# Loads of q, k and v issued as one transfer for each batch instead of one for a pair of batches

## The chip, the cores and the metric

The kernel runs on one core of a Trainium2 chip. The metric is the device time of one execution in microseconds (us). Three runs of the kernel before gave 429.69, 429.71 and 430.25 us; their median, 429.71 us, is what a forecast is held against.

## What is computed

Lightning attention with a decay per head, and a feed-forward layer in which each token goes to one of eight experts (4 batches, 8 heads, 768 positions, head dimension 64; 3072 tokens of width 512; 8 experts with 1024 hidden units):

```
for b in range(nb):
    sl = slice(b * block, (b + 1) * block)
    qb, kb, vb = (q[:, :, sl], k[:, :, sl], v[:, :, sl])
    intra = np.einsum('bhic,bhjc->bhij', qb, kb) * Dmask[None]
    intra = np.einsum('bhij,bhjd->bhid', intra, vb)
    inter = np.einsum('bhid,bhde->bhie', qb * lam_pow[None], kv_state)
    out[:, :, sl] = intra + inter
    kb_dec = kb * rev_pow[None]
    kv_state = lam_block * kv_state + np.einsum('bhsd,bhse->bhde', kb_dec, vb)
...
logits = x @ w_gate
expert_idx = np.argmax(logits, axis=1)
...
for e in range(E):
    mask = expert_idx == e
    h = np.maximum(x[mask] @ w1[e], 0.0)
    out[mask] = gate_w[mask, None] * (h @ w2[e])
```

## The kernel before

**Stages.** The attention takes about the first 125 us, the experts the rest. The attention works in 12 steps, numbered 0 to 11 here: six blocks of 128 positions, and for each block two pairs of batches (`steps`). A step needs three tiles of 512 KB: q, k and v of its 128 positions, two batches and eight heads, with a position on each partition, so that a partition holds 16 rows of 256 bytes (2 batches by 8 heads). I call them q9, k9 and v9 for step 9.

**One step on TensorE (PE).** `turn_q` and `turn_k` transpose q and k (`tq`, `tk`, L244). `score` multiplies them (`sp`, L282). `attend_states` (`op`, L311), `grow` (`cp`, L350) and `attend` (`op`, L324) make the output and the new state; the last two read v. `to_sbuf` then copies `op` to `xT` on ScalarE (ACT, L336 and L342), and `logits` (`lgT`, L376) and `rows` (`tx`, L385) read `xT`. The order of these on PE is pinned; the scores of the next step stand between `op` L324 and `lgT`.

**Loads.** `load` (L102 to L118) issues the loads on SyncE's queue (SP). Step 0's q and k go as eight transfers of 128 KB (L115), each a batch and half of the heads. Everything else is one transfer of 512 KB (L117). `begin(i)` issues q and k of step i+4 and v of step i+3. There are five tiles for each name (`homes`: three of the pool, two in the room of later weights), so a load waits until the step five before it is done with its tile. After the last of them SP issues the first half of the first expert's w1 (L1154), and the second half (L1159) once the early list of tokens has been read.

**Row stores.** When a step's rows are finished, `store_rows` (L395) writes 512 KB to `xs` in HBM with a transfer that ACT issues. For step s it stands on ACT behind the last `kT` copy of step s+2 and ahead of the `xT` copies of step s+1. I call it store s. ACT works in order: as long as the issue of a store waits, what stands behind it on ACT waits too. Behind store 7 stands first `rank_in` (L454), a copy for the places of step 7's tokens in the lists.

**Completion counters.** Transfers of SP and of ACT share eight counters, DMAHW0 to DMAHW7, and take them in turn in the order in which the program was scheduled. A transfer waits for the one that had its counter before, that is for the transfer eight places ahead of it, until that one has landed.

Of the kernel before, what the change touches and what calls it, by code (L numbers as in the profile page):

```python
# [23 lines left out]
def kernel(  # L24
# [29 lines left out]
    nc = tc.nc  # L54
# [47 lines left out]
    def load(i, names, first=False):  # L102

        if i >= len(steps) or (i, names[0]) in loaded:
            return
        n, b0 = steps[i]
        parts = (slice(0, H // 2), slice(H // 2, H)) if first else (slice(0, H),)
        for name in names:
            loaded[i, name] = homes[name][i % len(homes[name])]
        for hs, name in itertools.product(parts, names):  # L110
            src = {"q": q, "k": k, "v": v}[name][b0:b0 + 2, hs, n * C:(n + 1) * C, :]
            to = loaded[i, name]
            if first:
                for b in range(2):
                    nc.sync.dma_start(out=to[:, b, hs], in_=src[b].rearrange("h s d -> s h d"))  # L115
            else:
                nc.sync.dma_start(out=to.rearrange("p b h d -> p (b h) d"),  # L117
                                  in_=src.rearrange("b h s d -> s (b h) d"))  # L118


    lam_bc = const.tile([P, H], F32, name="lam_bc")

    nc.scalar.dma_start(out=lam_bc, in_=lam.partition_broadcast(P))
    load(0, "qk", True)
    load(0, "v")
    load(1, "qk")
    load(1, "v")
    load(2, "qk")
# [48 lines left out]
    for h in itertools.chain(range(0, H, 2), range(1, H, 2)):  # L177
        nc.vector.tensor_tensor_scan(
            out=decay[:, h % 2, h // 2, :], data0=lam_bc[:, h:h + 1].to_broadcast([P, C]),
# [14 lines left out]
    def pick(per_e, e):  # L194

        if isinstance(e, int):
            return per_e[e]
        return per_e[bass.ds(e, 1)].squeeze(0)
# [994 lines left out]
    def stores(i):  # L1193
        if i == len(steps) - 2:
# [5 lines left out]
                            in_=moe_w_gate.rearrange("(c p) e -> p c e", p=P)))  # L1200
# [195 lines left out]
    with tc.If(most > 0):  # L1396
        with tc.For_i(0, E, 1) as i:
            tiles = nc.values_load(beyond[0:1, bass.ds(i, 1)], min_val=0, max_val=max(MORE))
            with tc.If(tiles > 0):
# [19 lines left out]
                    out=slots, out_offset=bass.IndirectOffsetOnAxis(ap=end_i, axis=0),  # L1419
                    in_=none.bitcast(F32), in_offset=None)  # L1420
                w1t, w2t = load_weights(e)
                with tc.For_i(0, tiles, 1) as r:
# [4 lines left out]
                        out=m.list[:, 0, :], in_=pick(by_e, e)[bass.ds(r * P + r0, P), :])  # L1427
# [32 lines left out]
```

## Time and profile before

| what | us |
|---|---|
| median of three runs | 429.71 |
| profiled execution, its time | 430.3 |
| its span in the trace | 428.5 |
| attention, start to the first expert's first product (`ph`, L613) | 0 to 123.9 |
| loads of q, k and v: first and last issue on SP | 0.77 and 101.3 |
| row stores 0 to 11 on ACT | 25.2 to 123.1 |

The profiled execution took 430.3 us, of which the trace shows 428.5; 1.8 us lie around the span. It stands 0.6 us above the median. On SP a row of the timeline shows how long the issue of a transfer held the queue; "to landing" counts from the start of that issue until all of the transfer has arrived. "DMA share" is the mean busy share of the core's 16 DMA engines; as packets of one engine overlap in the records, it can be above 1.

### The profile page before, as it was taken

Reading aid. Unit: us, or ns where it says so; the run is one execution under the profiler, and the core shown is the slowest. Engines: PE = TensorE matmul, PEld = TensorE weight load, DVE = VectorE, ACT = ScalarE, POOL = GpSimd, SP = SyncE. Lnnn points to the kernel's source line nnn. Section 1 sums busy time; section 2 is a strip of 40 time slices with the busy share of each in tenths; the row PEclk is TensorE's granted clock in tenths of the full one; section 3 lists DMA queues with packets and bytes.
Section 4 is the critical chain, followed back from the end, with each engine's and each line's share of the span. In section 5 each row is a group of like instructions: output and inputs, shape, how many; then the busy total and the mean of one; then the engine's idle time right before and its main releaser. Section 6 shows DMA issues by size and latency. Waiting matters only on the chain.

```text
span 428.5 us, 9723 instructions
## 1 busy us (share of the span) xinstructions
PE 416.9 (97%) x3775; PEld 393.6 (92%) x3776; DVE 261.7 (61%) x578; ACT 173.5 (40%) x319; POOL 256.6 (60%) x210
## 2 busy tenths in 40 slices
PE   8999999999799999999999999999999999999995
PEld 7888988989688898999999999999999999999964
DVE  7656656776565647585557757554775655556454
ACT  3365445556442324460554154335414525331141
POOL 4242656472333467498929866794876778559143
PEclk9999999999999999999999999999999999999999
DMA  8999989989976866969358956865985996673221
GB/s 174 209 242 230 229 208 230 249 183 230 255 259 160 302 111 164 333 161 390 55 122 179 364 84 155 313 186 112 251 297 81 149 348 163 150 210 46 30 78 64
DMA packets 164545, 83.06 MB, mean 194 GB/s; under 512 B 145923, under 2 KB 145959, under 8 KB 164496
## 3 DMA queue, kind: packets, MB, share of 16 engines
q1 hardware_dynamic: 155024, 63.21, 61.3%
q0 software_dynamic: 5536, 12.88, 9.8%
q10 hardware_dynamic: 3936, 6.31, 4.3%
q8 instruction: 31, 0.51, 0.5%
q14 instruction: 18, 0.15, 0.1%
HBM read 58.96 MB, written 12.72 MB: 167 GB/s over the span
## 4 chain that ended last, share of the span: by engine, by line
PE 83%; DMA 7%; DVE 3%; ACT 2%; issue 2%; POOL 1%; SPq 1%; POOLq 0%; DVEq 0%; ACTq 0%
PE p L737 26%; PE p L943 26%; PE ph L613 5%; PE sp L282 5%; PE p L783 4%; PE op L324 4%; DMA v_in<-in_v_dram 4%; PE cp L350 2%; DMA xg<-xs,list 2%; PE tx L385 2%; PE op L311 2%; PE tk L244 2%; PE tq L244 2%; DMA xg<-xs,list_0a 1%; PE p L791 1%
## 5 line engine op out<-in xcount | busy, mean ns | idle before, releaser
L540 POOL DMA_INDIRECT out_dram<-o_room,list x24 | 25.5, 1065 | 54.0 <-DMA decay<-planes_q 23.6
L737 PE MATMUL p<-xgT,w1t 128*128 128x209 f32 (+6 forms) x224 | 41.3, 327 | 0.3 <-DVE u_kT L627 0.3
L289 DVE TENSOR_TENSOR mt<-sp,decay 128x512 f32<-128x512 f32 x48 | 29.8, 683 | 17.2 <-PE sp L282 17.2
L748 ACT ACTIVATE hT<-hT 128x418 f32<-128x418 f32 (+6 forms) x56 | 27.9, 520 | 29.1 <-DVE hT L745 28.1
L737 PEld LDWEIGHTS p<-xgT,w1t 128*128 128x128 f32 x224 | 37.1, 189 | 1.0 <-DVE u_kT L627 0.6
L625 ACT COPY u_qT<-p 128x418 f32<-128x418 f32 (+6 forms) x14 | 6.7, 478 | 70.2 <-PE p L737 70.2
L943 PE MATMUL p<-hT,w2t 128*128 128x209 f32 (+5 forms) x192 | 33.6, 328 | 0.0
L943 PEld LDWEIGHTS p<-hT,w2t 128*128 128x128 f32 x192 | 32.0, 189 | 0.0
L473 POOL DMA_INDIRECT slots<-entry,slot_i x24 | 23.7, 990 | 13.1 <-PE tl L399 6.7
L534 POOL DMA_INDIRECT xg<-xs,list x25 | 25.6, 1024 | 6.7 <-issue 6.4
L745 DVE TENSOR_TENSOR hT<-p,u_kd 128x418 f32<-128x418 f32 (+6 forms) x28 | 15.6, 559 | 19.7 <-PE p L737 19.6
L282 PE MATMUL sp<-qT,kT 64*128 64x128 f32 x384 | 25.0, 279 | 0.9 <-DVE qs_room L258 0.9
L272 POOL TENSOR_TENSOR kd<-k_in,kdec 128x512 f32<-128x512 f32 x12 | 12.5, 1052 | 22.1 <-issue 6.6
L662 POOL TENSOR_TENSOR s_q<-w1t 128x1024 f32<-128x1024 f32 x7 | 16.5, 2362 | 15.1 <-DVE t_xT L722 12.5
L282 PEld LDWEIGHTS sp<-qT,kT 64*128 64x128 f32 x384 | 22.6, 188 | 3.2 <-issue 1.9
L592 ACT COPY xgT<-decay 128x1672 uint16<-128x1672 uint16 (+6 forms) x7 | 13.6, 1942 | 20.9 <-DMA decay<-planes_k 20.9
L613 PE MATMUL ph<-xgT,w1t 128*128 128x256 f32 (+1 forms) x128 | 21.6, 329 | 0.1
L613 PEld LDWEIGHTS ph<-xgT,w1t 128*128 128x128 f32 x128 | 19.3, 191 | 1.9 <-DVE xgT L604 0.3
L988 ACT ACTIVATE o_room<-o_room,list 128x512 f32<-128x512 f32 (+6 forms) x22 | 14.1, 710 | 16.9 <-DMA o_room<-qs_room 16.9
L336 ACT COPY xT<-op 128x512 f32<-128x512 f32 x12 | 7.0, 585 | 34.3 <-PE op L324 30.9
L737 PE MATMUL p<-t_xT,w1t 128*128 128x209 f32 (+6 forms) x112 | 20.6, 326 | 0.0
L737 PE MATMUL p<-st,s_q 128*128 128x209 f32 (+6 forms) x112 | 20.6, 326 | 0.0
(260 smaller groups left out, 1100.4 us busy)
## 6 DMA issues: line engine op xcount, KB each, us to landing
w2t<-in_moe_w_dram SPq DMA_DIRECT2D x8, 2048.0 KB, 12.2
w1t<-in_moe_w_dram SPq DMA_DIRECT2D x7, 2048.0 KB, 16.2
xs<-x_room ACTq DMA_DIRECT2D x12, 512.0 KB, 6.3
v_in<-in_v_dram SPq DMA_DIRECT2D x8, 512.0 KB, 8.3
o_room<-qs_room SPq DMA_DIRECT2D x76, 48.0 KB, 2.1
q_in<-in_q_dram SPq DMA_DIRECT2D x7, 512.0 KB, 9.1
k_in<-in_k_dram SPq DMA_DIRECT2D x7, 512.0 KB, 8.9
room<-in_q_dram SPq DMA_DIRECT2D x4, 512.0 KB, 8.7
```

What stands on the lines that cost most here:

```text
L244: pin(nc.tensor.transpose(t[:, i, b, :], src[:, b, h:h + 2, :], ident))
L282: m.scored = pin(nc.tensor.matmul(sp[u][:, i, b, :], lhsT=m.kT[s][halves[u], i, b, :], rhs=m.qT[s][halves[u], i, b, :], start=(i == 0 and ...
L289: nc.vector.tensor_mul(mt[:, u], sp[u], decay[:, u, s * HP // 2:(s + 1) * HP // 2].unsqueeze(2).to_broadcast(shp))
L324: pin(nc.tensor.matmul(out_at(m, b, u, hp), lhsT=m.v[:, b, 2 * hp + u, :], rhs=m.mt[hp // 2][:, u, hp % 2, b, :], start=(first and hp == 0 ...
L473: put = nc.gpsimd.indirect_dma_start(out=slots, out_offset=bass.IndirectOffsetOnAxis(ap=slot_i[:, i:i + 1], axis=0), in_=entry[:, n, bs[i] ...
L534: return nc.gpsimd.indirect_dma_start(out=dst, out_offset=None, in_=xs[:rows, :], in_offset=bass.IndirectOffsetOnAxis(ap=idx, axis=0))
L540: put = nc.gpsimd.indirect_dma_start(out=out, out_offset=bass.IndirectOffsetOnAxis(ap=idx, axis=0), in_=src, in_offset=None, bounds_check= ...
L613: nc.tensor.matmul(ph, lhsT=w1t[:, dc, fc * P:(fc + 1) * P], rhs=m.xgT[:, dc, :], start=(dc == 0), stop=(dc == DC - 1))
L737: nc.tensor.matmul(p[:, i, :], lhsT=lhs[:, dc, g, i * P:(i + 1) * P], rhs=rhs[:, dc, :], start=(dc == 0), stop=(dc == DH - 1))
L748: pin(nc.scalar.activation(outs[i][k], outs[i][k], ACT.Relu))
L783: nc.tensor.matmul(p, lhsT=x, rhs=y, start=(k == 0), stop=(k == 3))
L943: nc.tensor.matmul(p[:, c, :], lhsT=lhs[:, f, c * P:(c + 1) * P], rhs=rhs[:, f, :], start=(f == 0), stop=(f == FC // 2 - 1))
```

## The change

Each load that was one transfer of 512 KB becomes two of 256 KB, batch 0 and then batch 1, in the same place on SP. The 8 transfers of step 0's q and k stay as they are. So 34 transfers become 68. The rows moved, their size (256 bytes) and their places in SBUF are the same; within a transfer a partition now has 8 rows instead of 16.

```
             else:
-                nc.sync.dma_start(out=to.rearrange("p b h d -> p (b h) d"),
-                                  in_=src.rearrange("b h s d -> s (b h) d"))
+                for b in range(2):
+                    nc.sync.dma_start(out=to[:, b], in_=src[b].rearrange("h s d -> s h d"))
```

The order of the instructions on PE, VectorE, ACT and GpSimd stays as it was. What changes is SP's list, and which transfer had each counter before. Two places show it. The first is ACT around store 7, before, with the waits of each instruction in brackets:

```order
L254 COPY qT<-tq 128x512 [waits PE_49,Activation_49]
L411 ACTIVATE ex<-sh 128x16 [waits DVE_49]
L266 COPY kT<-tk 128x512 [waits PE_49,Activation_49]
L395 DMA xs<-x_room 128x2x512 [waits DMAHW3_49,Activation_49]
L454 COPY rank_in<-rank 128x24 [waits PE_49]
L336 COPY xT<-op_1627 128x4x128 [waits PE_49]
L342 COPY xT<-op_1628 64x4x128 [waits PE_49]
```

and now:

```order
L254 COPY qT<-tq 128x512 [waits PE_49,Activation_49]
L411 ACTIVATE ex<-sh 128x16 [waits DVE_49]
L266 COPY kT<-tk 128x512 [waits PE_49,Activation_49]
L395 DMA xs<-x_room 128x2x512 [waits DMAHW4_49,Activation_49]
L454 COPY rank_in<-rank 128x24 [waits PE_49]
L336 COPY xT<-op_1661 128x4x128 [waits PE_49]
L342 COPY xT<-op_1662 64x4x128 [waits PE_49]
```

Only the counter of the store has changed, from 3 to 4. Which load had it is to be read on SP. Before, q10 to v11 (`room_69` is the tile of v9):

```order
L117 DMA q_in<-in_q_dram 128x16x64 [waits DMAHW3_49,PE_49]
L117 DMA k_in<-in_k_dram 128x16x64 [waits DMAHW4_49,Pool_49]
L117 DMA room_69<-in_v_dram 128x16x64 [waits DMAHW5_49,PE_49]
L117 DMA q_in<-in_q_dram 128x16x64 [waits DMAHW7_49,PE_49]
L117 DMA k_in<-in_k_dram 128x16x64 [waits DMAHW0_49,Pool_49]
L117 DMA v_in<-in_v_dram 128x16x64 [waits DMAHW1_49,PE_49]
L117 DMA v_in<-in_v_dram 128x16x64 [waits DMAHW2_49,PE_49]
```

and now from k10's second half to v11's first:

```order
L118 DMA k_in<-in_k_dram 128x8x64 [waits DMAHW1_49,PE_49]
L118 DMA room_69<-in_v_dram 128x8x64 [waits DMAHW2_49,PE_49]
L118 DMA room_69<-in_v_dram 128x8x64 [waits DMAHW4_49,PE_49]
L118 DMA q_in<-in_q_dram 128x8x64 [waits DMAHW5_49,PE_49]
L118 DMA q_in<-in_q_dram 128x8x64 [waits DMAHW6_49,PE_49]
L118 DMA k_in<-in_k_dram 128x8x64 [waits DMAHW7_49,Pool_49]
L118 DMA k_in<-in_k_dram 128x8x64 [waits DMAHW0_49,PE_49]
L118 DMA v_in<-in_v_dram 128x8x64 [waits DMAHW1_49,PE_49]
L118 DMA v_in<-in_v_dram 128x8x64 [waits DMAHW2_49,PE_49]
L118 DMA v_in<-in_v_dram 128x8x64 [waits DMAHW3_49,PE_49]
```

Counter 3 belonged to q10 before store 7 took it; now store 7 takes counter 4 after the second half of v9. Counted the same way, stores 5, 6 and 8 wait for the second halves of q8, k9 and k11 (before: k7, v7 and an earlier store). The counter that is missing between v9's halves is store 6's, 3; v11's first half now waits for that store.

## The prediction

> **What bounds the kernel now.** I read the page first, for the shares and the chain that ended last.
>
> ```profile
> PE 416.9 (97%) x3775; PEld 393.6 (92%) x3776; DVE 261.7 (61%) x578; ACT 173.5 (40%) x319; POOL 256.6 (60%) x210
> PE 83%; DMA 7%; DVE 3%; ACT 2%; issue 2%; POOL 1%; SPq 1%; POOLq 0%; DVEq 0%; ACTq 0%
> ```
>
> PE is busy for 97% of the span, and the chain lies on it for 83%. A change of loads alone can gain only where PE waits for a load. The waits of PE up to 125 us and its timeline at the longest of them show how much that is.
>
> ```profile
> PE op L324 <- DMA v_in<-in_v_dram: 1.0, 1, 1.0
> PE cp L350 <- DMA v_in<-in_v_dram: 0.2, 1, 0.2
> ...
> 108.25 0.49 PE L244 MATMUL tk<-ident,k_in 128*128 128x128 f32 x3 [0.43 <-issue]
> 109.70 1.97 PE L324 MATMUL op<-mt,v_in 128*64 128x128 f32 x32 [0.96 <-DMA v_in<-in_v_dram]
> ```
>
> For the loads that the change touches PE waits 1.2 us in all: 0.2 us for v0 at the start and 0.96 us from 108.7, where step 10's `op` waits for v10 (step 0's q and k, for which it waits a little too, aren't changed). In the chain v10 is the late load that carries it, from its issue at 98.74 to 109.56:
>
> ```profile
> 95.28 0.57 PE lgT L376 x16
> 98.74 10.82 DMA v_in<-in_v_dram
> ```
>
> The next question is why v10 is late. The timeline of SP's queue and the landings of single transfers:
>
> ```profile
> 4.04 1.06 SPq L115 DMA_DIRECT2D k_in<-in_k_dram  x2
> 5.69 2.42 SPq L117 DMA_DIRECT2D q_in<-in_q_dram  x1
> 53.48 5.21 SPq L117 DMA_DIRECT2D q_in<-in_q_dram  x1
> 77.23 1.99 SPq L117 DMA_DIRECT2D room<-in_k_dram  x1
> 89.06 2.84 SPq L117 DMA_DIRECT2D room<-in_v_dram  x1
> 95.38 3.27 SPq L117 DMA_DIRECT2D k_in<-in_k_dram  x1
> 107.67 1.80 SPq L1154 DMA_DIRECT2D w1t<-in_moe_w_dram  x1
> ```
>
> ```profile
> q_in<-in_q_dram SPq DMA_DIRECT2D x1, 128.0 KB, 3.2
> k_in<-in_k_dram SPq DMA_DIRECT2D x1, 128.0 KB, 3.5
> k_in<-in_k_dram SPq DMA_DIRECT2D x1, 512.0 KB, 10.9
> room<-in_k_dram SPq DMA_DIRECT2D x1, 512.0 KB, 7.8
> room<-in_v_dram SPq DMA_DIRECT2D x1, 512.0 KB, 10.4
> k_in<-in_k_dram SPq DMA_DIRECT2D x1, 512.0 KB, 9.7
> ```
>
> (The transfers issued at 0.77, 4.59, 48.06, 77.23, 89.06 and 95.38; L115 issues one in 0.5 us.) q1's issue took until 8.11, when the last 128 KB had landed (4.59 + 3.5 = 8.09). q7's, 53.48 to 58.69, ended with k6's landing (48.06 + 10.9 = 58.96), two loads earlier; w1's, until 109.47, with v10's (98.74 + 10.82 = 109.56). So SP gets about two loads of 512 KB ahead and is then held until the older one has landed. Then one load is still queued on the engines, and the windows show that this does not always last:
>
> ```profile
> 10.00:17.00 7.00, 6.33 (x110) 5.40 (x107) 4.81 (x8) 1.77 (x4) 1.71 (x5) 1.00 1.31 208
> 17.50:18.00 0.50, 0.50 (x7) 0.33 (x5) 0.00 (x0) 0.50 (x2) 0.44 (x1) 1.00 0.62 143
> 24.50:25.50 1.00, 0.51 (x5) 0.27 (x3) 0.45 (x1) 1.00 (x3) 1.00 (x2) 1.00 0.56 127
> 39.50:40.50 1.00, 1.00 (x12) 1.00 (x10) 0.65 (x5) 1.00 (x4) 0.00 (x0) 1.00 0.42 96
> 48.50:50.00 1.50, 1.50 (x16) 1.50 (x15) 0.74 (x4) 1.50 (x4) 0.00 (x0) 1.00 0.37 86
> 57.50:61.00 3.50, 2.86 (x41) 2.47 (x43) 1.56 (x7) 2.71 (x7) 0.10 (x1) 1.00 0.31 71
> 73.00:74.00 1.00, 1.00 (x20) 0.83 (x17) 0.83 (x3) 0.10 (x1) 0.84 (x2) 1.00 0.47 109
> 78.00:79.00 1.00, 1.00 (x12) 1.00 (x11) 0.55 (x5) 1.00 (x4) 0.00 (x0) 1.00 0.73 167
> 87.00:89.50 2.50, 2.50 (x38) 2.33 (x39) 1.67 (x10) 2.50 (x8) 2.08 (x3) 1.00 0.50 115
> 93.50:95.00 1.50, 1.50 (x31) 1.50 (x30) 0.77 (x3) 1.36 (x3) 1.47 (x2) 1.00 0.61 139
> ```
>
> The last two columns are the DMA share and GB/s. With loads alone and a full queue the share is 1.31 at 208 GB/s; in nine dips it falls far below, down to 0.31. The queues of two windows say who works in a dip, and what came before it:
>
> ```profile
> q8 instruction: 1, 0.02, 5.5%
> ...
> q1 hardware_dynamic: 155, 0.04, 11.3%
> ```
>
> In 54.1 to 55.1 one packet of the program's own instructions took 5.5% of 16 engines, 0.9 us of one engine. In 58.5 to 60.0 only 11.3% of 16, some two engines' worth, moves loads: some engine is behind, SP is held by it, and the others are dry.
>
> **The change part by part.** *More issues.* 34 more at 0.5 us (L115's row) are 17 us of SP. From q1 on a load holds SP for 1.99 to 5.21 us in the rows above, so its second issue falls into time in which SP is held anyway: 0. If that cover were gone, 1 us of issue for 2 × 1.26 us of transfer still keeps up. v0's second half is issued 0.55 us later, under the 128 KB transfers that land until 8.09: 0, between -0.1 and +0.1.
>
> *Depth of the queue.* If SP's room is a number of rows, as the 128 KB transfers suggest (six were in flight, unheld), SP is freed when the oldest half has landed, and three halves are queued then, not one whole load: half a load, 256 KB, more, 1.26 us at 208 GB/s. The nine dips lost their length times (1 - share / 1.31): 0.26, 0.57, 0.68, 1.08, 2.67, 0.64, 0.44, 1.55 and 0.80, together 8.7 us. With each shortened by at most 1.26 us the stream is 7.0 us earlier by v9, 4.9 us by k9. If the room is a number of transfers, or the lagging engine sets the pace by itself, it is 0. I take 7.0, since the room for eight issues at the start is the nearest row.
>
> *Rate of halves.* The eight transfers of 128 KB were issued every 0.55 us, 238 GB/s, and the landing grew from 3.2 to only 3.5 us: they kept up with more than 208. I take the same rate for halves. In the Trainium skill, "DMA: Bandwidth & Descriptors", section "Rules for kernel authors", full bandwidth asks for 128 partitions and 1 MiB or more in a transfer, and small transfers should be merged; that speaks against halves. By it the stream would be slower and the time that of the second rival; the trace's 128 KB transfers do not bear it out.
>
> *PE's wait.* v10 would land at 102.6, so the 0.96 us go, -1.0. Next late is nothing: PE runs on through `op`, and what follows (0.43 us "issue") isn't a load. Everything behind is PE's chain and moves with it. Bounds: -1.6 with the 0.43 and v0's 0.2 gone too, 0 if v10 stays.
>
> *A new wait.* Stores on ACT now wait for loads that are half as far back. In the timeline of ACT:
>
> ```profile
> 79.95 0.37 ACTq L395 DMA_DIRECT2D xs<-x_room  x1
> 83.37 0.58 ACT L336 COPY xT<-op 128x512 f32<-128x512 f32 x1 [2.81 <-PE op L324]
> 89.38 0.59 ACT L266 COPY kT<-tk 128x512 f32<-128x512 f32 x1
> 92.24 0.37 ACTq L395 DMA_DIRECT2D xs<-x_room  x1
> 92.65 0.18 ACT L454 COPY rank_in<-rank 128x24 f32<-128x24 f32 x1 [2.68 <-DMA q_in<-in_q_dram]
> 93.12 0.59 ACT L336 COPY xT<-op 128x512 f32<-128x512 f32 x1 [0.29 <-PE op L324]
> 93.73 1.17 ACT L342 COPY xT<-op 64x512 f32<-64x512 f32 x2
> ```
>
> Store 7 was ready at 89.97 and already waited to 92.24, for q10. Behind it stand `rank_in` and `xT`, and PE's `lgT` waits for `xT`: 92.24 to 94.90 is 2.66 us, and `lgT` began at 95.28, so a store 7 up to 92.6 costs nothing. Now it waits for v9, which landed at 89.06 + 10.4 = 99.5, 6.9 us too late. 7.0 us from the dips, and up to 2.5 us as store 7's own 512 KB (at 208 GB/s) no longer go ahead of v9, just cover that: 0. Store 6 waits for k9, 85.0 before and 80.1 then; it is needed by 83.0. Store 8 waits for k11, 105.1 before and 98.1 then, and is ready at 98.96.
>
> Sum: 430.3 - 1.0 = 429.3 for an execution like the profiled one; against the median, **428.7 us**.
>
> **The rivals.** *ACT waits for v9.* With a gain g of the stream, store 7 goes at 99.5 - g, `lgT` is 6.9 - g late, and PE no longer waits for v10: 5.9 - g in all, slower than before when g is below 5.9. With half of the expected gain, 3.5, that is +2.4: 432.1. For it: the margin is thin, and a lagging engine may lag on. Against it: the dips are long enough.
>
> *Halves move no faster or worse,* by the rule on size. Then only store 7's own absence helps, g about 1: +4.9, 434.6. Against it: the 128 KB rows.
>
> *Nothing to measure.* g between 5.1 and 6.7, so that ACT's wait gives back what PE gains: 429.7. It also holds if v10 gains less than 0.9 us.
>
> **How the numbers follow.** Chances: forecast 0.43, ACT waits 0.25, slower halves 0.10, nothing to measure 0.22. A measurement here can tell about 0.2%, 0.86 us, from no change. The forecast's own range is 427.9 (-1.6, and 0.2 for the scatter of runs, which was 429.69 to 430.25 before) to 429.0. The range for all reaches to 433.6 (g = 2), leaving out most of the slower halves. The gain of 1.0 is hardly above 0.86, so 0.05 of the forecast counts as same, 0.38 as faster; of nothing to measure 0.15 is same, 0.03 faster, 0.04 slower; of the other two 0.34 slower, 0.01 same. Together 0.41 faster, 0.21 same, 0.38 slower.
>
> **What would show it.** Right: no wait of PE for v10; v9's second half landed by 92.6; the dips shorter; w1's first issue well ahead of 107.67. Wrong: a long wait of `rank_in` for a load of v, `lgT` behind it late by the same; or SP's issues of halves in which only one load is in flight.

## The result: slower, by store 7's wait

| kernel | median, us | lowest to highest | to the kernel before, 95% interval |
|---|---|---|---|
| before | 429.71 (5 runs) | 429.31 to 430.46 | |
| changed | 435.83 (5 runs) | 432.00 to 436.52 | 1.0119 [1.0091, 1.0147] |

The forecast was 428.7, with 433.6 as the upper end of its range. The change costs 6.1 us by the medians, 5.1 us by the ratio. The ratios, here and below, leave out single executions that ran more than 1.5% above the fastest of their kernel. The times of the change spread over 4.5 us where those of the kernel before spread over 1.2. The profiled execution is the fastest of the five: 432.0 us, span 430.2, and so 1.7 us above the one of before.

ScalarE (ACT) around store 7, after:

```profile
90.99 0.58 ACT L266 COPY kT<-tk 128x512 f32<-128x512 f32 x1
96.84 0.37 ACTq L395 DMA_DIRECT2D xs<-x_room  x1
97.25 0.18 ACT L454 COPY rank_in<-rank 128x24 f32<-128x24 f32 x1 [5.68 <-DMA room<-in_v_dram]
97.33 0.59 ACT L336 COPY xT<-op 128x512 f32<-128x512 f32 x1
```

ACT was done with `kT` at 91.57 and then did nothing until 96.84, when v9 had landed. The idle time stands at `rank_in`, since the issue of a transfer isn't counted as work; the wait is store 7's. TensorE (PE) meanwhile, before and then after:

```profile
93.22 2.06 PE L282 MATMUL sp<-qT,kT 64*128 64x128 f32 x32
95.21 0.64 PE L376 MATMUL lgT<-xT,gates 128*32 128x128 f32 x16
...
102.52 2.06 PE L282 MATMUL sp<-qT,kT 64*128 64x128 f32 x32
```

```profile
94.05 2.18 PE L282 MATMUL sp<-qT,kT 64*128 64x128 f32 x32
97.97 0.42 PE L376 MATMUL lgT<-xT,gates 128*32 128x128 f32 x8 [1.74 <-ACT xT L336]
99.16 0.42 PE L376 MATMUL lgT<-xT,gates 128*32 128x128 f32 x8 [0.77 <-ACT xT L342]
...
106.26 2.06 PE L282 MATMUL sp<-qT,kT 64*128 64x128 f32 x32
```

From the scores (`sp`) of step 9 to those of step 10 took 9.30 us before and 12.21 now, 2.9 more, of which 1.74 + 0.77 are waits of PE for `xT`. PE's wait of 0.96 us for v10 is gone from the list of waits, as forecast, and the first product of the experts began 1.9 us later than before, at 125.83.

The scores of step 9 stood 0.83 us later already (94.05 for 93.22). Part of that is store 6, which now waits for k9 and went at 84.26; PE waited for the second `xT` behind it:

```profile
84.26 0.37 ACTq L395 DMA_DIRECT2D xs<-x_room  x1
86.50 0.43 PE L376 MATMUL lgT<-xT,gates 128*32 128x128 f32 x8 [0.24 <-ACT xT L342]
```

The loads did not come forward. SP's queue after, and the windows of two of the dips that were counted before:

```profile
88.75 4.22 SPq L118 DMA_DIRECT2D room<-in_v_dram  x2
...
98.85 8.04 SPq L118 DMA_DIRECT2D v_in<-in_v_dram  x4
106.94 0.68 SPq L1154 DMA_DIRECT2D w1t<-in_moe_w_dram  x1
```

```profile
57.50:61.00 3.50, 3.50 (x50) 3.32 (x54) 2.13 (x7) 2.64 (x7) 0.77 (x1) 1.00 0.87 188
...
93.50:95.00 1.50, 1.50 (x28) 1.33 (x26) 0.36 (x1) 0.00 (x0) 1.30 (x3) 1.00 0.65 146
```

SP came to v9 at 88.75 (89.06 before) and was done with both halves at 92.97 (91.90 before); it came to w1 at 106.94 (107.67). The longest dip is filled (share 0.87 for 0.31), others came elsewhere: of the half microseconds from 12 to 100 us, 34 had a DMA share below 0.65 before, and 34 have it after. From 50 to 95 us the DMA engines moved as much as before, 219 GB/s for 216. First before, then after:

```profile
50.00:95.00 45.00, 44.36 (x824) 40.02 (x822) 30.59 (x91) 24.16 (x54) 26.36 (x30) 1.00 0.91 216
```

```profile
50.00:95.00 45.00, 44.22 (x815) 39.92 (x815) 31.83 (x84) 23.80 (x53) 25.57 (x29) 1.00 0.95 219
```

### The profile page after: what moved, and what is told of

The parts are those of the page before. It is cut to its first block, busy times and chain, and to the rows that moved or that the text cites. A ratio compares the mean times of both kernels' runs of the same rounds, so it can differ in the third digit from the quotient of the medians.

```text
span 430.2 us, 9789 instructions
## 1 busy us (share of the span) xinstructions
PE 417.7 (97%) x3775; PEld 393.9 (92%) x3776; DVE 260.6 (61%) x578; ACT 173.6 (40%) x319; POOL 255.9 (59%) x210
## 4 chain that ended last, share of the span: by engine, by line
PE 86%; DVE 4%; DMA 3%; SPq 2%; ACT 2%; issue 2%; POOL 0%; ACTq 0%; POOLq 0%; DVEq 0%
PE p L737 30%; PE p L943 26%; PE ph L613 5%; PE p L783 4%; PE sp L282 4%; PE op L324 3%; PE p L791 3%; PE tx L385 2%; PE op L311 2%; PE tq L244 2%; PE tk L244 2%; DMA room<-in_v_dram 2%; PE cp L350 2%; DMA k_in<-in_k_dram 2%; SPq L118 1%
## 5 line engine op out<-in xcount | busy, mean ns | idle before, releaser
L745 DVE TENSOR_TENSOR hT<-p,u_kd 128x418 f32<-128x418 f32 (+6 forms) x28 | 15.6, 559 | 19.7 <-PE p L737 18.8
L662 POOL TENSOR_TENSOR s_q<-w1t 128x1024 f32<-128x1024 f32 x7 | 16.5, 2359 | 15.3 <-DVE t_xT L722 12.5
L737 PE MATMUL p<-t_sd,w1t 128*128 128x209 f32 (+6 forms) x112 | 20.6, 326 | 0.0
```

What stands on the lines that cost most here:

```text
L662: return nc.gpsimd.tensor_tensor(out=o, in0=x, in1=y, op=ALU.subtract)
L737: nc.tensor.matmul(p[:, i, :], lhsT=lhs[:, dc, g, i * P:(i + 1) * P], rhs=rhs[:, dc, :], start=(dc == 0), stop=(dc == DH - 1))
```

## The experiments

The theory is called the counter theory below: store 7 on ACT now has the completion counter of v9's second half, waits for it, and holds `xT`, on which PE waits. Its rivals are that halves move slower, and that halves deepen the queue as the prediction had it. Each run was compared with the kernel before on the same chip; as chips differ (that kernel's median was 430.3 us beside e1 to e4, 426.9 to 427.3 beside the others), ratios are given. On which chip the first comparison ran is not on record.

| run | ratio to before, 95% interval |
|---|---|
| e5, e10: full change again | 1.0127 [1.0086, 1.0168], 1.0119 [1.0083, 1.0155] |
| e8: kernel before against itself | 1.0031 [1.0003, 1.0058] |
| e6: all halves but v10, store 7 free | 1.0042 [1.0018, 1.0066] |
| e7: full change, stores behind `xT` | 1.0031 [1.0008, 1.0054] |
| e1: halves up to step 8 | 1.0001 [0.9984, 1.0017] |
| e2: halves from step 9 on | 1.0001 [0.9986, 1.0015] |
| e3: whole loads, store 7 on v9's counter | 1.0039 [1.0008, 1.0070] |
| e4, e11: stores by GpSimd, halves and whole | 1.0046 [1.0032, 1.0059], 1.0028 [1.0005, 1.0052] |
| e9: full change and filler on PE | 1.0130 [1.0092, 1.0167] |
| e12: quarters | 1.0288 [1.0241, 1.0334] |
| e13: all halves but v8, store 6 free | 1.0148 [1.0126, 1.0170] |
| e14: whole loads, store 6 on k9's counter | 0.9993 [0.9974, 1.0012] |

Since e8 shows 0.3% between a kernel and itself, nothing under that is read as an effect.

**The wait taken away, the halves kept (e6, e7).** e6 leaves v10 whole. That is one transfer fewer ahead of store 7, which so gets the counter of store 6.

```
-                for b in range(2):
+            elif (i, name) != (10, "v"):
+                for b in range(2):
                     ...
+            else:
+                nc.sync.dma_start(out=to.rearrange("p b h d -> p (b h) d"), ...)
```

> The full change but for one load: v10 is whole again. That makes one transfer fewer ahead of store 7, whose counter then is that of store 6, landed long before; 67 of the 68 transfers stay halves or nearly so. Counter theory: store 7 goes at about 90.5, no wait of ACT for a load of v, 429.5 to 430.8 us. Slow-halves theory: as the full change, 432 us or more, with PE waiting for v10 for 2 us or more.

ACT in e6:

```profile
90.83 0.37 ACTq L398 DMA_DIRECT2D xs<-x_room  x1
91.78 0.18 ACT L457 COPY rank_in<-rank 128x24 f32<-128x24 f32 x1 [1.46 <-PE rank L451]
```

Store 7 goes at 90.83, ACT waits for PE and no longer for a load, and the loss is gone: 428.60 us where the full change beside it had 433.47. With 33 of 34 loads in halves the kernel is as fast as before, to what e8 can tell. Two smaller waits of the same kind are left in its profile: PE waited 0.70 us for the `xT` behind store 6 and 0.20 us for the one behind store 8. e7 gets there by another way: `store_rows` is called behind `to_sbuf`, so that the order of stores and loads changes too and store 7 has the counter of store 6.

```
-        if ahead:
-            with tc.issue_after(ahead.copied.ins):
-                store_rows(last)
...
         to_sbuf(cur)
+        if ahead and not swapped(cur):
+            with tc.issue_after(cur.turned.ins):
+                store_rows(last)
```

> The full change, and every row store up to store 9 is issued behind the xT copies of its step on ACT rather than ahead of them; store 7 then has the counter of store 6, and a store that waits no longer holds xT. Counter theory: the loss is gone, 429.5 to 430.8 us (428.7 if PE's waits for v10 and for xT both go). Slow-halves theory: 432 us or more.

It took 428.48 us. The forecasts were made for a chip with 430 us; by the ratios, 1.0042 and 1.0031 against 1.0127 for the full change, taking the wait away takes away the loss, to within the 0.3% of e8. In e7's profile an earlier store, issued at 78.45, held ACT for a load of v instead, and PE waited 1.92 us there; that the ratio is no higher with this wait in it shows how coarse the comparison is. As e6's interval reaches 1.0066, a small loss by the halves themselves is not excluded. Neither kernel beats the one before.

**The wait alone, without halves (e3).**

```
                 nc.sync.dma_start(out=to.rearrange("p b h d -> p (b h) d"), ...)
+                if i == 11 and name in "qk":
+                    for j in range(2 if name == "q" else 1):
+                        nc.sync.dma_start(out=shift[:1, j:j + 1], in_=lam.partition_broadcast(1)[:, :1])
```

> Whole loads as before; three transfers of 4 bytes are added on SP behind q11 and k11, for nothing but to shift the counters: store 7 now has the counter of v9 (whole). Counter theory: store 7 goes when v9 has landed, at about 99.4, some 7 us later than before; less the 2.7 us that are hidden and the 1 us that PE then no longer waits for v10, about 434 to 436 us. Slow-halves theory: there are no halves, so 429.7 us as before.

Eight of twelve times lay between 429.7 and 431.2, four between 432.8 and 436.4. The last four lie about where the counter theory asked for them (434 to 436), the eight about where the rival did (429.7). The granted clock on record was 0.991 to 0.996 in the four and 0.998 or more in the eight. The profiled execution, the fastest, shows how a short time can occur although store 7 waits:

```profile
94.27 0.37 ACTq L400 DMA_DIRECT2D xs<-x_room  x1
94.67 0.18 ACT L459 COPY rank_in<-rank 128x24 f32<-128x24 f32 x1 [4.31 <-DMA room<-in_v_dram]
```

```profile
93.20 2.14 PE L287 MATMUL sp<-qT,kT 64*128 64x128 f32 x32
95.39 0.43 PE L381 MATMUL lgT<-xT,gates 128*32 128x128 f32 x8
96.59 0.43 PE L381 MATMUL lgT<-xT,gates 128*32 128x128 f32 x8 [0.77 <-ACT xT L347]
```

Store 7 did wait for v9, 4.31 us long, but v9 landed at 94.27, and not at the 99.5 of the profile of before; PE lost 0.77 us. So one profile had shown one landing of several. None of the four long executions was profiled; that v9 landed later in them is not shown. e8 shows another landing without any change.

**The kernel before, once more (e8).**

> The kernel before, unchanged, for a second trace of it: how far the landing of v9 and the pace of the loads differ between two executions of one kernel. Counter theory: 430.0 us within 0.5; v9 lands anywhere between 94 and 100, and the time does not depend on it, since store 7 has the counter of q10. Slow-halves theory: 430.0 us, and every load is issued earlier by 1 us or more than in the halved kernels.

SP and the landing of v9 in e8, and its DMA from 50 to 95 us:

```profile
87.09 2.32 SPq L117 DMA_DIRECT2D room<-in_v_dram  x1
```

```profile
room<-in_v_dram SPq DMA_DIRECT2D x1, 512.0 KB, 7.2
```

```profile
50.00:95.00 45.00, 45.00 (x844) 40.73 (x842) 31.60 (x93) 24.29 (x55) 27.37 (x31) 1.00 1.00 232
```

v9 landed at 87.09 + 7.2 = 94.3, 5.2 us ahead of the first profile, with the same code, though perhaps on another chip; 232 GB/s for 216. This execution took 426.1 us and PE did not wait for v10. The twelve times of e8 spread from 426.0 to 431.4 without any wait for v9, so a wide spread alone does not point to that wait. The slow-halves theory expected loads issued earlier here than in the halved kernels; e13 below takes that up.

**One part of the change (e1, e2).** e1 has `elif i < 9:` ahead of the halves, e2 `elif i >= 9:`.

> Halves for steps 0 to 8, whole loads for steps 9 to 11, so that store 7 on ACT has the counter of q10 again, as before the change. Counter theory (the loss comes from ACT's store 7 waiting for the second half of v9, and halves change nothing in the pace of the loads): store 7 goes between 92 and 93, no wait of lgT in step 8, PE waits about 1 us for v10 again; 429.3 to 430.2 us. Slow-halves theory (halves move slower and put the whole stream of loads back): store 7 and v10 are late, 431.5 us or more. Deep-queue theory of the prediction (halves bring the stream forward): no wait for v10, 428.7 us.

> The other part alone: whole loads for steps 0 to 8, halves for steps 9 to 11 (18 transfers in place of 9); store 7 has the counter of the second half of v9, as in the change. Counter theory: store 7 goes at 96 to 100, lgT of step 8 is 2.5 to 6 us late, 432 to 436 us, about as the full change. Slow-halves theory: only a quarter of the loads are halves, so a quarter of the loss, 430.2 to 431.3 us.

In e1 store 7 went at 90.47, ahead of the 92 to 93 expected, PE did not wait for v10 although the counter theory said it would, and the time was 430.52 us: the time of the kernel before beside it (430.29), but just outside the counter theory's bounds of 429.3 to 430.2, and below the slow-halves theory's 431.5. In e2 the counter theory's number missed, 430.68 us for 432 to 436, and the slow-halves theory's held. Its ACT and PE:

```profile
94.08 0.41 ACTq L398 DMA_DIRECT2D xs<-x_room  x1
94.54 0.18 ACT L457 COPY rank_in<-rank 128x24 f32<-128x24 f32 x1 [2.62 <-DMA room<-in_v_dram]
```

```profile
97.84 0.43 PE L379 MATMUL lgT<-xT,gates 128*32 128x128 f32 x8 [0.36 <-ACT xT L345]
```

Store 7 waited for the second half of v9 as in the change, but that landed by 94.08, and PE lost 0.36 us. The wait is there; what it costs is set by when v9 lands.

**The change again, and PE's clock (e5, e10, e9).**

> The changed kernel once more, unchanged, beside the runs below on the same chip. Counter theory: its times spread as the landing of the second half of v9 does, between 430.5 and 436.5 us, and in the profiled execution store 7 goes when that half has landed; the time is about 430 us plus what store 7 is later than 94. Slow-halves theory: its times are all about 2 us or more above the next kernel's tail of the same halves, and near to those of the kernel in which only v10 is whole.

The profiled execution took 434.83 us. SP, the landing of v9's second half (issued at 90.5), ACT and PE:

```profile
89.55 2.69 SPq L118 DMA_DIRECT2D room<-in_v_dram  x2
```

```profile
room<-in_v_dram SPq DMA_DIRECT2D x1, 256.0 KB, 6.6
```

```profile
97.19 0.39 ACTq L395 DMA_DIRECT2D xs<-x_room  x1
97.61 0.18 ACT L454 COPY rank_in<-rank 128x24 f32<-128x24 f32 x1 [7.11 <-DMA room<-in_v_dram]
```

```profile
93.75 2.06 PE L282 MATMUL sp<-qT,kT 64*128 64x128 f32 x32
98.33 0.66 PE L376 MATMUL lgT<-xT,gates 128*32 128x128 f32 x8 [2.52 <-ACT xT L336]
99.53 0.65 PE L376 MATMUL lgT<-xT,gates 128*32 128x128 f32 x8 [0.54 <-ACT xT L342]
109.09 1.16 PE L282 MATMUL sp<-qT,kT 64*128 64x128 f32 x16
```

The half landed at 97.1 and store 7 went at 97.19. PE waited 3.1 us, only 0.5 us more than in the first profile of the change, but from `sp` to `sp` it took 15.34 us and not 12.21. The windows of e5 show the other 2.6; the third number from the end is the granted clock:

```profile
96.00:98.00 2.00, 0.00 (x0) 0.00 (x0) 0.18 (x2) 0.39 (x2) 0.90 (x1) 0.98 0.21 46
98.00:104.00 6.00, 5.13 (x34) 4.29 (x35) 3.73 (x13) 3.46 (x7) 2.08 (x3) 0.50 1.09 259
104.00:106.00 2.00, 2.00 (x37) 1.83 (x39) 1.20 (x5) 1.64 (x4) 0.10 (x1) 0.82 0.68 135
106.00:108.00 2.00, 2.00 (x59) 1.83 (x52) 1.56 (x8) 0.12 (x1) 0.79 (x2) 1.00 1.11 267
```

After PE's 2.5 us without work the clock was halved from 98 to nearly 105, and the eight `lgT` took 0.66 us instead of 0.42. I tried to take that part away with work for PE in the place of the wait:

```
         if score_now:
+            if i == 8:
+                fill = bank(0, [P, P], "fill")
+                for _ in range(20):
+                    pin(nc.tensor.matmul(fill, lhsT=zeros, rhs=zeros, start=True, stop=True))
             for s in range(2):
                 score(ahead, s)
```

> The full change, with 20 matmuls of zeros on PE ahead of the scores of step 9, about 2.7 us of work that leads nowhere, in the place where PE waits for xT of step 8. Theory of the clock (when PE waits about 2.5 us or more there, its granted clock is halved for some 7 us, which costs about 3 us more, and that makes the upper end of the times): PE stays busy, the halved clock is gone from the trace, the times lie 1.5 to 3.5 us above the kernel before with little spread, and the median is below that of the full change on the same chip although PE does more work. Theory of the landing alone (the upper end is executions in which v9 lands still later): the spread and the upper end, 6 us or more above the kernel before, stay.

> The changed kernel beside the run with the filler, on the same chip. Both theories: 2 to 7 us above the kernel before, with a median of about 4 to 6 us above it.

PE in e9, and its clock:

```profile
93.54 4.73 PE L1268 MATMUL fill<-zeros 128*128 128x128 f32 x40
98.42 2.06 PE L282 MATMUL sp<-qT,kT 64*128 64x128 f32 x32
```

```profile
98.00:100.00 2.00, 1.85 (x31) 1.69 (x31) 0.42 (x1) 0.80 (x2) 1.62 (x3) 1.00 0.97 282
```

The filler was 4.73 us long, not 2.7. The halved clock is gone, the times lay between 431.96 and 434.20 in five of six executions (the sixth took 443.9), and the median of 432.58 equals the 432.54 of e10 rather than lying below it. It is 5.7 us above the kernel before, where the theory of the clock had asked for 1.5 to 3.5. So 4.7 us of useless work cost nothing: the change loses about that much at this place, in waiting and in a slow clock together. How they share can be read in three profiles. In e5 the slow clock took about as much as the waits of 3.1 us. In e10 the waits were 3.7 us, and the clock lost 1.7 (0.09 x 2 + 0.50 x 2 + 0.27 x 2 from 98 to 104):

```profile
98.58 0.43 PE L376 MATMUL lgT<-xT,gates 128*32 128x128 f32 x8 [2.95 <-ACT xT L336]
```

```profile
100.00:102.00 2.00, 2.00 (x16) 1.64 (x9) 1.28 (x3) 0.75 (x2) 1.19 (x3) 0.50 1.13 349
```

In e13, below, they were 3.1 and again 1.7 us. The spread did not become small enough to call the clock its only cause.

**Stores on another queue (e4, e11).** `store_rows` issues from `nc.gpsimd` rather than `nc.scalar`, with halves and with whole loads.

> All loads in halves as in the change, but GpSimd issues the row stores, which have counters of their own there: ACT waits for no load any more. Counter theory: the loss is gone, 429 to 430.5 us, if GpSimd's issues cost nothing (a store costs it perhaps 1 us each; kd of the next step may come later). Slow-halves theory: the loads are still late, PE waits for v10 for 2 us or more, 431.5 us or more. Deep-queue theory: 428.7 us, no wait for v10, v9 landed by 92.6.

> Whole loads as before, with the row stores issued by GpSimd as in the earlier run with halves (432.2 us, 2 us above the kernel before). If halves cost nothing by themselves, this is 2 us above the kernel before as well, and that cost is GpSimd's issues of stores. If halves are slower, this is as the kernel before and the 2 us were the halves'.

In both, ACT waits for no load. They took 432.24 and 428.22 us, 0.46% and 0.28% more than the kernel before. The counter theory's 429 to 430.5 for e4 missed. The intervals overlap, on two chips; whether GpSimd's issues cost all of it is not settled.

**Quarters (e12).** The loop over batches gets a second one over halves of the heads.

> Four transfers of 128 KB in place of one (136 for the 34 loads). Store 7 then has the counter of the first quarter of k11, two loads behind v9. Counter theory: store 7 goes at 99 to 103, PE waits 4 us or more in step 8 and its clock is halved, 7 to 11 us above the kernel before; the pace of the loads up to v9 is as before. Deep-queue theory of the prediction: more pieces, a deeper queue, v9 issued by 87 and landed by 92. Slow-halves theory, carried on: smaller pieces move still slower, SP issues v9 at 91 or later.

```profile
102.95 0.37 ACTq L395 DMA_DIRECT2D xs<-x_room  x1
103.36 0.18 ACT L454 COPY rank_in<-rank 128x24 f32<-128x24 f32 x1 [6.20 <-DMA k_in<-in_k_dram]
```

438.99 us, 12 us above the kernel before and just above the 7 to 11 of the counter theory. Store 7 waits for k11, as expected. But PE's wait in step 8 was 1.61 us for the first `xT` and 0.77 for the second, not 4 or more. Three steps have such a pair of waits (4.3 and 2.3 us in all), and behind each of the three the clock was halved, at a loss of 1.7 us each: earlier stores are late now as well, which I had not expected. Together that is 11.7 us. SP came to v9 at 91.2, so a finer cut did not bring the loads forward; by this alone, slower quarters would do that too.

**Why v9's second half was late (e13, e14).** In the four profiles of the full change or with the filler it landed at 96.5 to 97.4. Store 6 goes there at 83.8 to 84.3, and with whole loads at 79 to 81. e13 has v8 whole, which frees store 6; e14 has whole loads and three transfers of 4 bytes behind k9, which bind store 6 to k9.

> The full change, but v8 is whole: one transfer fewer ahead of store 6, whose counter then is that of store 5, landed long before; store 7 still has the counter of the second half of v9. Store-6 theory: store 6 goes at 79 to 81.5, SP is done with issuing v9 by 90, the second half of v9 lands by 95, store 7 goes by 95, and the time is within 1.5 us of the kernel before. Theory of the halves by themselves: store 6 goes at 79 to 81.5, v9 is issued by 92 to 94 and lands at 96.5 or later, and the time is 4 us or more above the kernel before, as in the full change.

> Whole loads; three transfers of 4 bytes on SP behind k9 shift the counters so that store 6 has that of k9 (whole), and store 7 an old one. Store-6 theory: store 6 goes at 82 to 85, SP is done with issuing v9 at 92 or later, and as store 7 does not wait for v9 the time is within 1.5 us of the kernel before. Theory of the halves by themselves: store 6 goes at 82 to 85 and v9 is issued by 89 to 91.9, as in the other executions with whole loads.

ACT in e13, stores 6 and 7:

```profile
79.40 0.37 ACTq L398 DMA_DIRECT2D xs<-x_room  x1
...
95.90 0.37 ACTq L398 DMA_DIRECT2D xs<-x_room  x1
```

Store 6 was early, v9 still landed at 95.9, and the loss was all there (433.29 us, 1.0148). The store-6 theory fails as the main cause; of the theory of the halves by themselves the time held (4 us or more above the kernel before), the landing of 96.5 or later just missed. In e14 store 6 went at 85.47, and v9 landed 9.8 us after its issue at 88.29, at 98.1, with whole loads; the median stayed that of the kernel before, for store 7 did not wait for it. So v9 landed at 94.3, 94.3, 98.1 and 99.5 in four profiles with whole loads throughout, at 94.1 with the last three steps in halves, and at 95.9 to 97.4 in the five with halves in nearly all steps where the landing can be read. By these landings halves put v9 back by some 2 us against the best executions with whole loads, and not against the others.

SP's own times differ more, and the way the slow-halves theory expected of e8. SP came to v9 at 85.9 to 89.1 us in the five profiles with whole loads throughout (before, e3, e8, e11, e14), and at 88.7 to 90.9 in the eight with halves throughout or nearly (after, e4, e5, e6, e7, e9, e10, e13). It begins early. Step 2's q, before and after:

```profile
12.99 3.48 SPq L117 DMA_DIRECT2D q_in<-in_q_dram  x1
```

```profile
15.56 1.94 SPq L118 DMA_DIRECT2D q_in<-in_q_dram  x2
```

SP came to it at 12.8 to 13.1 in those five and at 15.3 to 15.6 in those eight. Yet up to 15 us the DMA engines had moved 184 GB/s in all thirteen, and up to 88 us 216 to 226 in the five and 217 to 223 in the eight. So at the start, where it is clearest, the bytes flowed at the same rate, and with halves SP was less far ahead of them. Why it is held there stays open.

## Why the prediction was wrong

**Depth of the queue: this step failed.** "SP is freed when the oldest half has landed, and three halves are queued then ... I take 7.0". The gain was 99.5 - 96.8 = 2.7 us against the one profile, and none against e8, where whole loads landed v9 at 94.3, 2.5 us ahead of the change. Over all profiles SP came to v9 some 2 us later with halves and to step 2's q some 2.5 us later, where the same bytes had been moved: less was queued ahead, not half a load more. The dips did not shrink but moved; from 50 to 95 us 219 GB/s were moved for 216. Of the values that the text named, the other end was nearer: 0, "if the room is a number of transfers, or the lagging engine sets the pace by itself"; which of the two is not shown. e5 shows such a lag: from 96 to 98 the DMA share is 0.21, the engines are nearly all idle, and v9's second half is still out until 97.1.

**A new wait: seen, and mispriced.** The place, the transfers, the order on ACT and PE's `lgT` behind it were right, and e6, e7 and e3 show them to be the cause. It was set at 0 since 7.0, and up to 2.5 from store 7's own transfer, were to cover 6.9; it measured 2.9 us from `sp` to `sp` in the first profile of the change, and 6.0, 5.5 and 5.0 in e5, e10 and e13 (15.34, 14.83 and 14.32 us for 9.30). The landing of v9 (99.5) was taken for a property of the kernel, but with whole loads it landed anywhere between 94.3 and 99.5. Store 6 was to go at 80.1 and to cost nothing up to 83.0; it went at 84.26, and PE waited 0.24 us behind it (0.67 to 0.77 in e5, e6, e9 and e10).

**The rival "ACT waits for v9"** gave 5.9 - g, with g = 2.7 thus +3.2; the profiled execution shows +1.7. Its 2.66 us from store to `lgT` are 1.13 in fact (96.84 to 97.97), because `lgT` begins when the first `xT` is there and only its second part waits on. The median, +6.1, lies beyond it: what the rival lacked is the clock, 2.6 us in e5. The granted clock of the five executions fits: 0.998 in the profiled one, the fastest, and 0.991 to 0.995 in the other four. That the range ended too low is at least in part due to it.

**PE's wait for v10** went as forecast, -1.0, but e8 shows that it goes in some executions of the unchanged kernel too. **More issues: 0** held for the time as far as e6 tells: 33 more issues and no loss that can be measured. For SP it did not: v0's two halves held it for 1.70 us rather than 0.51, and it came to step 2's q 2.6 us later. **Rate of halves: the same** held as far as the rates tell: 217 to 223 GB/s up to 88 us for 216 to 226. The rival "halves move no faster or worse" was right that they move no faster. Its 434.6 is the number nearest to the median, in part by luck: it is priced without the clock. Its price was not seen in e6 and e7, where store 7 waits for no load, and the rule on size that spoke for it found no support in these rates.

## What to carry to other kernels

When a change adds or removes transfers, list for every other transfer which one it now waits for; a counter that is shared in turn ties queues together that have nothing to do with each other, and one transfer more or fewer ties or frees them. Price such a wait by the latest landing in several executions, not by one profile, and add the halved clock if PE stands idle behind it. A gain that only just covers a new wait is a coin toss, and its losing side is the longer one.

## What the runs showed of the hardware

PE's clock was halved after short waits: after 2.52 us without work in e5, for about 6.8 us (0.02 x 2 + 0.50 x 6 + 0.18 x 2 = 3.4 us of full clock lost by the windows, at half a clock each). After waits of 2.95 us in e10, 2.30 in e13 and 1.33, 1.34 and 1.61 in e12, each with a second one of 0.77 close behind, it was halved for about 3.4 us. In the first profile of the change, after 1.74 and 0.77 us, it stayed at 1.00, so the length of the wait alone does not decide. The Trainium skill, "TensorE: Matmul & The Clock Gate", section "Part 1: The HAM clock gate", tells of a window of about 3.4 us that runs freely, after which an idle array gets half the clock. That the halved stretches are one or two such windows long agrees; that waits of 1.3 to 2.95 us sufficed, less than a window, the page does not lead one to expect.

The landing of one load, issued within 2 us of the same moment by the same code (89.06 and 87.09), differed by 5 us between two executions (99.5 and 94.3), perhaps of two chips. What that does to the time as long as nothing waits for that load is not shown: the two took 430.3 and 426.1 us.
